# Two attentions under a gate on one Trainium2 core: the memory tokens handed on by a transpose, crosswise moves and one add

## Chip, cores and metric

One core of a Trainium2 chip (trn2). The metric is the time of one execution on the device in microseconds (us), as the median of several runs, and the kernel before and the changed kernel are compared on the same chip.

## The reference, cut to what matters

```python
g = sigmoid((x * gate_w).sum(-1, keepdims=True))           # x: 1 x 2048 x 512
a = A(x, mem0, Wq, Wk, Wv, Wo)
b = B(x, wq, wk, wv, wo, beta)
return g * a + (1 - g) * b

def A(...):                  # 32 heads of 128, M = 8 memory tokens, segments of 32 tokens
    mask = (idx[:, None] < M) | (idx[:, None] >= idx[None, :])      # over 40 tokens
    mem = mem0
    for s in range(64):
        h = concatenate([mem, x[:, 32 * s : 32 * s + 32]], axis=1)  # 40 tokens
        q, k, v = h @ Wq, h @ Wk, h @ Wv                            # 512 -> 32 x 128
        p = softmax(where(mask, q @ k.T / sqrt(128), -1e9))
        o = (p @ v) @ Wo                                            # 32 x 128 -> 512
        mem = o[:, :8]                                              # goes into the next segment
        outs.append(o[:, 8:])
...
def B(...):                  # 32 heads of 16, 4 segments of 512
    # causal softmax inside a segment, plus a linear memory (M, z) carried on
    # from segment to segment, mixed by sigmoid(beta); then @ wo
```

Attention A is a recurrence: a segment's first eight output rows are the next segment's memory tokens. Attention B and the gate depend on x alone.

## The kernel before

**A planned program.** The Python code does not emit instructions directly. Its class `Prog` collects operations, each with an engine (or a choice of engines), what it reads and writes, a cost in us and a priority. `schedule()` then replays a fixed list, the string `ORDER` at the head of the file: for every engine the sequence of its operations, found beforehand by the planner's own search over those costs (`LATENCY`, `TO_PE`, `FETCH`, `FLOOD` and the others). The list also says which engine an operation with a choice goes to. PSUM's eight banks are given out in that order; semaphores and waits are derived afterwards. So what stands in front of what on an engine is set by `ORDER`.

**Tilings of TensorE.** Most matmuls work on column groups of 32: four matmuls side by side, each on 128 x 32 weights, which the trace shows as `128*32`, in quadruples (x4). Others work on rows of 16 or 32 (`16*128`, `32*128`) or on the full array. `mm` (L1024, L1026) takes the form that fits the work before it.

**Attention A, one segment (`p_seg`).** `hT` holds the segment's 32 columns: 24 new tokens of x, copied by GpSimd (L1441), and 8 memory tokens. The last 8 tokens of each segment, the "rest", depend on no memory for their projections; they are projected for four segments at once (`p_rest`, `p_xr`) and fetched per segment.

- `wproj` (L1401) projects k, q and v in halves of 16 heads (r = 0, 1): 16 matmuls of 512 columns each half.
- k and q go out of PSUM to `st` (L1001, the general copy helper, on ScalarE or VectorE) and are transposed by VectorE (L1466) into `KT` and `QT`. v goes to `V_sb` directly.
- `p_s` makes the scores of half r in one bank, for four heads on each partition group: first the causal mask by a matmul of `neg` with `hide` over 224 columns (a L1024 x4), then 16 matmuls of 40 columns (L1481) and 4 for the rest keys (L1485) on top of it. The bank and the tile `PT` hold 4 x 40 columns and behind them 4 x 16 columns of the rest.
- L1489 takes the exponential, `p_u` sums by a matmul with ones (L1504), takes the logarithm and the exponential of its negative (L1508, L1510: 1 / sum), and multiplies (L1512 on VectorE, L1515 for the rest, mostly on GpSimd).
- L1546 and L1555 multiply the probabilities with v, giving `OT_sb`.

**The output projection (`wo`, L1300).** 64 matmuls of 256 columns collect o @ Wo in one bank. For head h, l = h mod 4 and q = l mod 2; half d of the 512 output columns goes to partitions 64 q + 32 d. So partitions 0 to 63 hold the sum over heads of even l, partitions 64 to 127 that over odd l, each as two halves of 256 columns of 32 tokens. What follows:

```python
self.copy(part, lambda: pb[so.b][:, 0:256], 256, [so], rhl, "par%s" % name, prio)   # L1001, 128 x 256 f32
...
ins = self.mm(pe, m, pb[so.b][:, 256 + 16 * c:272 + 16 * c], part[:, 128 * c:128 * c + 128], self.fold[:, :], True, True)
...
d.tensor_copy(mem[0]..., pb[so.b][:, 256:288]...)      # hm, L1323: into hT's memory columns, bf16
...
d.tensor_tensor(ao[:, :], pb[so.b][0:64, 0:256], part[64:128, :], ALU.add)     # row, L1330
```

`part` is a copy of the whole bank in SBUF. The fold, 8 matmuls of 16 columns in float32 with `fold` (a 0/1 matrix), adds the two halves, takes the eight memory tokens and turns them, in one step; each of them is two records in the trace (L1024 x16). `hm` then writes them into the next `hT`. `row` adds the halves for the output rows, and a DMA brings them to `a_rows` in DRAM (`ast`); `p_tail` reads 128 rows back, mixes them with b by the gate and writes the output. `p_orest` runs the same projection for the rest tokens of four segments, with no fold.

**Attention B** is cut into small pieces that `ORDER` strews between A's steps: logits (`bL`, L1141), exponentials (L1159, ScalarE), the causal cut (L1165, GpSimd), values (`bPV`, L1182), transposes (L1218) and so on.

**The start (`p_init`, `p_x`).** SyncE's queue holds x's four pieces first, then B's weights and A's weights; ScalarE's queue has `wBk`. The gate is 64 matmuls of one column (L934).

Of the kernel before, what the change touches and what calls it, by code (L numbers as in the profile page):

```python
# [15 lines left out]
    "c-nPZ31CcD7e061Oy<p&$t1+u5JZVctf6X;*g}I^N)<sBRiw3+Q2dR3S4)G|zLXR#B0`BqiG7c~qNOPk$;3>OH}Agx-Z#rzqQlI*dGFqH&+?t`oO{XDTA>uUH~uhX23k})eZf2@Z"  # L16
    "=DSjR>Fb@c?X-fd|dB!<4Fr&P3v_0bJkX{uoV}d{O!c0dD$mAo@mi)>MywyR%jf4<EI6^*Yx|iJ*!Id(%|=XP`CI}=%b3JkN5>OA1+<<2>jr?p+@*}-t5ta^w{)RSkiZgG5$ic-C"
    "^IucXeX3TJ`>FdU77?1ifJ1-QB5&-2<WR38onUu*q{Wq3OvEu;!2hVJ$3emO1rAcI%cy-)qR6hr~0jH<W?4-W>=E$_aS_Ax~=fY5W1sh6ROY^}ZRvTy0dLL=VoQt8e0+#Q+A!eam"
    "mF_Cv&t6Jy{zi0<eB(1Z9o1ku5VqR$W4afo3oE*Ch@Ld$@H3#~QqTYKZLouT%DCceSYJ8<Ks&x1;N9bd83$wr^DF!?MvmZadCFX2hZ18_k2+WwO80}y{iJE|1vI4dy{Ir2ia1?*k"
    "FP%vG5*AFh`)@=8NnCc#T7)p8{2I#Njbli?Ht<MlCV0E_2Lgd>Reicq#{zej<2(WYtcaYcfL=mzo<b^n`oQrt?4X=l0K|A;jYSjkffA_2MFVM6SfEMX^o@in&({YaCYOW$y`)p7D"  # L20
    "S`XiW8t_aqvKqjW{{7CHnNq!}ps?b<?`R*wI}B4o9BGDCQx}lccl|wAQsx#w{o02*@C?H*nhOpKFwQr|H)O2w?}{*(xL7i>^Ow;17;L=E6Uiuf7ORCqgCn5CVV*y)c>XNdyXQC&8"
    "+Y72_;!n^%v+zWkK>Q@Ko%!kq_yRP(Z#qJVwdIw8L)k~B$+4;xv_U_r96XPubB_I5D2!~a2}dp1JvLq@gWDhOdm=<**9v?sxJW25Ym?-ldeoxX!x`4-3l+>aiqjY*kKt=fdyyMrS"
    "TtKi`-Q|l8k2%X9cZ`c^&x5D1fH0$}`K-Y19{9|K0owjuuA~MQY~T9tV}(4D~NG=u6&MiY&(Y)ds*WfKih3Y5+XW8~DJ8n4rAi61zX|fPX3h>*sPY#?253SEIsV1Hk8!_{Fs%!nQ"
    "XbL@>yhz*P#id{eO=GyuC3I7pc!iC#F>x^|MNu9I~d942j2BKs}C{32?UUb0LFQ0ix-*wE`Wywhw40;SaxR(xH&0w&1~3r>%^+Q~*1w%X0dLK`~oRiUZ%v@YZ{<={$P$O>#Ht-g5"
    "W_?5ZV8Q)X6FKfa2uH#n*1->#gx`OOrGTS3=MBIgi05c@<lVI(bMKO(!P|IwkpyRX!0q9ky<A$_0F>qr~Z`i)*Pf7ko@^0+Ebu=O`6HS4D0zHsqF%|pCbq*x&7jftOc|B(>)Ul5$"
    "KZkl{cAySxd)nCa4`?xYI8Ydc-J`?j)*Ub>l_L53X(X=*iUSH*O)~7hZzt}07vPzsz=lT9d}LFYhY-VCz%g-Sk&Tdn#%}I-!r0;ryuSkmW=ndEhe6SCNkfQele4rTz@yN|bXC7X5"
    "{J?2%yvEGvj;w-nk4KLC-en4_WIY7iDIe*l{w;mHRx|tg>Hls*GGYd1hEQaKs1Q}WW<p1#~=%4@4Jyoy%+bJlSOafyRp_Xa4`#}?irSp1pk9MQq0GYpf9%!-z_SyD|7gBZ%B5TIq"
    "j09gbnawgKX$c#?|1Cs~gEHo!)LH84CffGH0VZT0$^?t^N$w830B|hK2#$tvh^^sW`y7ue)i_0Lx#2>;^cu>5W;-xd<!l97zIn;Kf(ek&7pZQ+7YB*SmTARuV{y-AwMMCKM1LYPP"
    "~))4IWaaGge4THwmP{^wvY!*lvJH(bT~67Xw$Rb#i-yJ6bZqrpAMCqpVq+CL^KX1>vZdW9hs0a&MX{9>MDOZ)R2yhq84)`!GpUJj{u>>cvyS0!<>j?=fe0?v}Q=Z<x@?wNUY$yZA"
    "zFPco@wd?LO2?m!oCp7uI?No{xf`T7mh(Vuka2P2NBjL6@&q4tn9-LUHbLvQ<mFTs0mU8w)fQ=)Tg95Y{pjmMvz9MhukU!<q>{^889C|HXya@J>msYn;Tl_Dv*39cH1&mo+Xe41Y"  # L30
    "-wSm-uVZSP0nU3c{&z|2*8u<9e)|_x{U6>^pl7v3#2Y5&Q0%_`roFvjdeSO!h*#aoFJaTRlWAg97R_;xOeeX3z-(9QdN}SDbR{UFCKc&eeOa*yIPK9s9P}2;t504CtmqX2Mw+iQ5"
    "@tKA=UflNik^qvi@F+4>L0)d(&!xk19$q(bRtIQWc@BSEx8e4y#yo$@6;zSCHbBOeZ<h6B!k<!-TSDxi4K*bikZ>pp~bl>Hqu#;4C5khfUzc#d<{t6?Px5m@jG!{EB_;XNdZ7Qa<"
# [1584 lines left out]
```

## Time and profile before

| | |
|---|---|
| median of 3 runs | 831.91 us (829.27 to 833.25) |
| the profiled execution | 832.89 us |
| its span in the trace | 831.2 us |
| PE (TensorE matmul) busy | 809.5 us, 97%, 24474 records |
| DVE (VectorE) busy | 617.3 us, 74% |
| ACT (ScalarE) busy | 562.9 us, 68% |
| POOL (GpSimd) busy | 260.9 us, 31% |
| granted TensorE clock | 0.998 |

A line such as `L1001 DVE CAST V_sb<-pb 128x512 bf16<-128x512 f32 x65 | 44.5, 685 | 9.9 <-PE pb L1401 9.0` is a group: the line of the kernel, the engine, the operation, the tile written and the tile read, their shapes, the count; busy us in all and mean ns of one; and the idle time of that engine just before these instructions, with what released them. PEld is TensorE's loading of weights, which runs beside the matmuls. A line of the chain of waits gives start, length, engine, tile, line and count.

### The profile page before, as it was taken

The page shows a single profiled execution, that of the slowest core. Times are in us where ns is not written, and L with a number is a line of the kernel's source. Part 1 is how long each engine was busy: PE and PEld are TensorE (multiplying, and loading weights), DVE is VectorE, ACT ScalarE, POOL GpSimd, SP SyncE. Part 2 cuts the span into 40 slices and gives each one's busy share as a digit, 9 for nine tenths or more (in the row PEclk, how much of TensorE's full clock was granted, in tenths as well). Part 3 has the DMA queues.
Part 4 walks back from the last instruction along what each step waited for, and adds up shares of the span by engine and source line. Part 5 has one row for each costly group of instructions (what it writes and reads, how often), then busy time and mean ns, then how long its engine had stood idle before and what let it go on. Part 6 is the DMA issues. An engine that isn't in the chain of part 4 may idle for free.

```text
span 831.2 us, 53272 instructions
## 1 busy us (share of the span) xinstructions
PE 809.5 (97%) x24474; PEld 521.5 (63%) x24474; DVE 617.3 (74%) x1398; ACT 562.9 (68%) x1278; POOL 260.9 (31%) x576
## 2 busy tenths in 40 slices
PE   9999999999999999999999999999999999999987
PEld 4445666666666566666666666666766665666654
DVE  4688667768778768678676687776878767886776
ACT  3577676777766667776667766676656677767663
POOL 3443231323322332323233233423232223323340
PEclk9999999999999999999999999999999999999999
DMA  9983111121111111111011111100111100000001
GB/s 341 414 247 52 40 24 43 43 45 27 43 28 28 39 28 44 27 34 44 15 47 46 38 27 31 40 14 18 44 42 32 39 20 15 13 23 23 22 21 36
DMA packets 71701, 45.63 MB, mean 55 GB/s; under 512 B 50046, under 2 KB 69942, under 8 KB 69942
## 3 DMA queue, kind: packets, MB, share of 16 engines
q1 hardware_dynamic: 70422, 41.18, 17.5%
q8 instruction: 192, 3.15, 1.6%
q10 hardware_dynamic: 1056, 1.05, 0.4%
q14 instruction: 31, 0.25, 0.1%
HBM read 30.72 MB, written 8.87 MB: 48 GB/s over the span
## 4 chain that ended last, share of the span: by engine, by line
PE 87%; DVE 4%; ACT 3%; DMA 2%; issue 1%; SPq 1%; POOL 0%; DVEq 0%; POOLq 0%
PE pb L1401 47%; PE pb L1300 17%; PE pb L1024 7%; PE pb L1141 4%; PE pb L1026 2%; PE pb L1546 2%; PE pb L1182 2%; DMA st<-in_A_mem_dram 2%; PE pb L1504 2%; PE pb L1481 1%; PE pb L1230 1%; PE pb L1555 1%; DVE KT_sb L1466 1%; PE pb L1485 1%; ACT rc_sb L1510 1%
## 5 line engine op out<-in xcount | busy, mean ns | idle before, releaser
L1001 ACT ACTIVATE st<-pb 128x512 bf16<-128x512 f32 (+2 forms) x313 | 149.0, 494 | 103.0 <-PE pb L1401 78.0
L1159 ACT ACTIVATE PTB<-pb 128x640 bf16<-128x640 f32 x240 | 158.4, 703 | 37.2 <-PE pb L1141 32.5
L1401 PE MATMUL pb<-Wv_sb,hT 128*32 128x512 bf16 x2048 | 162.8, 381 | 0.2 <-DVE ao L1330 0.2
L1401 PE MATMUL pb<-Wq_sb,hT 128*32 128x256 bf16 (+1 forms) x3072 | 138.0, 308 | 0.1
L1300 PE MATMUL pb<-Wo_sb,OT_sb 128*32 128x256 bf16 x4096 | 132.8, 273 | 3.0 <-issue 1.9
L1401 PE MATMUL pb<-Wk_sb,hT 128*32 128x512 bf16 x2048 | 132.0, 379 | 0.1
L1300 PEld LDWEIGHTS pb<-Wo_sb,OT_sb 128*32 128x32 bf16 x4096 | 100.7, 96 | 18.4 <-ACT OT_sb L1001 4.3
L1165 POOL TENSOR_SCALAR_AFFINE_SELECT PTB<-PTB 128x512 bf16<-128x512 bf16 x120 | 77.6, 647 | 107.4 <-ACT PTB L1159 100.8
L1515 POOL TENSOR_TENSOR PT_sb<-PT_sb,rc_sb 128x64 bf16<-128x64 bf16 x90 | 33.1, 367 | 248.9 <-ACT rc_sb L1510 240.5
L1401 PEld LDWEIGHTS pb<-Wq_sb,hT 128*32 128x32 bf16 x3072 | 82.5, 97 | 39.1 <-issue 0.8
L1466 DVE STREAM_TRANSPOSE QT_sb<-st 128x256 bf16<-128x256 bf16 (+1 forms) x192 | 94.4, 510 | 16.7 <-ACT st L1001 15.1
L1466 DVE STREAM_TRANSPOSE KT_sb<-st 128x512 bf16<-128x512 bf16 x128 | 89.4, 700 | 11.6 <-ACT st L1001 9.5
L1001 ACT ACTIVATE OT_sb<-pb 128x320 bf16<-128x320 f32 (+1 forms) x140 | 58.1, 428 | 37.9 <-PE pb L1555 36.3
L1401 PEld LDWEIGHTS pb<-Wk_sb,hT 128*32 128x32 bf16 x2048 | 57.0, 97 | 42.4 <-ACT PTB L1159 1.1
L1001 DVE CAST OT_sb<-pb 128x320 bf16<-128x320 f32 (+1 forms) x120 | 56.8, 478 | 31.3 <-PE pb L1555 29.3
L1401 PEld LDWEIGHTS pb<-Wv_sb,hT 128*32 128x32 bf16 x2048 | 52.2, 98 | 18.8 <-DVE ao L1330 0.7
L1508 ACT ACTIVATE rc_sb<-pb 128x160 f32<-128x160 f32 x128 | 38.8, 303 | 36.3 <-PE pb L1504 35.3
L1323 DVE CAST hT<-pb 128x32 bf16<-128x32 f32 x63 | 12.0, 191 | 66.4 <-PE pb L1024 66.1
L1489 ACT ACTIVATE PT_sb<-pb 128x224 bf16<-128x224 f32 x128 | 45.6, 356 | 17.4 <-PE pb L1485 12.8
L1001 DVE CAST V_sb<-pb 128x512 bf16<-128x512 f32 x65 | 44.5, 685 | 9.9 <-PE pb L1401 9.0
L1512 DVE TENSOR_TENSOR PT_sb<-PT_sb,rc_sb 128x160 bf16<-128x160 bf16 x128 | 42.7, 334 | 8.2 <-ACT rc_sb L1510 6.7
L1001 ACT ACTIVATE stg<-pb 128x512 bf16<-128x512 f32 (+1 forms) x68 | 37.9, 559 | 14.3 <-PE pb L1401 10.2
(203 smaller groups left out, 1472.3 us busy)
## 6 DMA issues: line engine op xcount, KB each, us to landing
Wv_sb<-in_A_Wv_dram SPq DMA_DIRECT2D x4, 1024.0 KB, 11.8
Wk_sb<-in_A_Wk_dram SPq DMA_DIRECT2D x4, 1024.0 KB, 21.0
Wq_sb<-in_A_Wq_dram SPq DMA_DIRECT2D x4, 1024.0 KB, 26.9
Wo_sb<-in_A_Wo_dram SPq DMA_DIRECT2D x4, 1024.0 KB, 20.9
rest_v<-stg SPq DMA_DIRECT2D x112, 32.0 KB
rem_v<-rest_v SPq DMA_DIRECT2D x28, 128.0 KB, 2.6
a_rows<-ao SPq DMA_DIRECT2D x63, 32.0 KB
stg<-a_rows SPq DMA_DIRECT2D x15, 128.0 KB
```

The lines of the kernel that those rows point to most:

```text
L1001: self.P.op(("act", "dve"), (lambda a: a.activation(dst, src(), ACT.Copy), lambda d: d.tensor_copy(dst, src())), reads=reads, writes=write ...
L1024: ins = pe.matmul(out[32 * c:32 * c + 32], lhsT[:, 32 * c:32 * c + 32], rhs, start=start, stop=stop, tile_position=(0, 32 * c), **kw)
L1141: ins = pe.matmul(pb[slot.banks[i]][:, base + a - lo:base + b - lo], KT[r0:r1, 128 * kc:128 * kc + 128], Q[r0:r1, t0 + a:t0 + b], start=Tr ...
L1159: P.op("act", (lambda dst=dst, src=src: lambda a: a.activation(dst, src(), ACT.Exp, scale=0.25))(), reads=[pair], writes=["%s%d_%d" % (nam ...
L1165: P.op("gp", (lambda pt=pt, ii=ii: (lambda g: g.affine_select(pt, pt, ([[0, len(ii)]] if len(ii) > 1 else []) + [[1, 128]], ALU.is_ge, 0.0 ...
L1300: ins = pe.matmul(pb[so.b][p0:p0 + 32, 0:256], tok(r, g, l), self.Wo[:, h, 256 * d:256 * d + 256], start=(r == 0 and g == 0 and l < 2), st ...
L1401: ins = pe.matmul(self.pb[sl.b][32 * g:32 * g + 32, 0:hi - lo], x[:, c, 0:32], cols, start=(c == 0), stop=(c == C - 1), tile_position=(0, ...
L1466: op("dve", (lambda dst=dst, src=src: lambda d: d.transpose(dst, src))(), reads=["st%d%s" % (i, tag)], writes=["%sT%d%s" % (kind, r, tag)] ...
L1489: op("act", lambda a: a.activation(PT[:, r, :], pb[rb.b][:, 0:224], ACT.Exp, scale=SCALE), reads=[rb], writes=["PT%d" % r, "PT%dr" % r], n ...
L1508: op("act", lambda a: a.activation(rc[:, r, :], pb[rb.b][:, 0:160], ACT.Ln), reads=[rb], writes=[rr], name="ln%d_%d" % (s, r), cost=t_act( ...
L1512: op("dve", lambda d: d.tensor_tensor(PT[:, r, 0:160], PT[:, r, 0:160], rc[:, r, :], ALU.mult), reads=[rp, rr], writes=[rp], name="nrm%d_% ...
L1515: op(("dve", "gp"), tuple((lambda e: e.tensor_tensor(rest, rest, late(rc[:, r, :]), ALU.mult)) for _ in range(2)), reads=[rp + "r", rr], w ...
```

## The change

The fold and its matrix are gone. In `wo` the two halves' columns are now taken in blocks of 32 (block index 4 bits: c, e, d; d says which half of the partitions a column goes to), and for the memory projections of odd l the order of e is reversed. VectorE transposes the bank's 128 x 256 in blocks of 32 x 32 (`turn`) into the tile `rc`, which holds 1 / sum at other times. Two `swap` copies bring 64 partitions x 32 elements each from one half of the partitions to the other, on ScalarE or GpSimd, and one VectorE add (`hm`) sums the halves into `hT`. The copy `par` now has 64 partitions in place of 128 and a priority 0.2 later; `row` adds blocks, and `p_tail` puts the columns back in order.

The mask has 160 columns in place of 224: in the scores' bank and in `PT` each head has 56 columns now, 16 of the rest and 40 of its own, and the mask is written over the 40. All readers use strided views.

x's DMAs have the first priority in the planner, `wB` loads 384 of 512 columns, the gate is 64 matmuls of 128 columns on column groups and a transpose, costs and latencies of the planner are set anew, and `ORDER` is a new list.

```diff
-    LATENCY = {"pe": 0.22, "act": 0.04, "dve": 0.04, "gp": 0.1, "sp": 2.0}
-    TO_PE = {"pe": 0.0, "act": 0.015, "dve": 0.06, "gp": 0.05, "sp": 0.0}
+    LATENCY = {"pe": 0.25, "act": 0.05, "dve": 0.05, "gp": 0.1, "sp": 2.0}
+    TO_PE = {"pe": 0.0, "act": 0.07, "dve": 0.08, "gp": 0.09, "sp": 0.0}
...
-        self.gw = t("gw_sb", [128, C])
+        self.gw = t("gw_sb", [128, C, 32])
...
-        self.hide = t("hide_sb", [128, 224])
+        self.hide = t("hide_sb", [128, 160])
...
-        self.fold = t("fold_sb", [128, 16], F32)
...
-            dma(self.g_wB[k], (lambda k: lambda s: s.dma_start(self.wB[k], self.B_w[k].rearrange("(c p) n -> p c n", p=128)))(k),
-                writes=["wB" + k], name="dma_wB" + k, prio=-102 if k == "k" else -99, load=dict(k=3.0, q=2.0, v=1.5)[k], cost=0.5, ring=4.0,
+            dma(self.g_wB[k], (lambda k: lambda s: s.dma_start(self.wB[k][:, :, 0:384], self.B_w[k].rearrange("(c p) n -> p c n", p=128)[:, :, 0:384]))(k),
+                writes=["wB" + k], name="dma_wB" + k, prio=-102 if k == "k" else -99, load=dict(k=2.7, q=1.0, v=1.0)[k], cost=0.5, ring=4.0,
...
-                  writes=[rs], name="dma_x%d_%d" % (sb, i), prio=prio - 1.5, load=0.4, cost=0.45 if sb or i else 1.2)
+                  writes=[rs], name="dma_x%d_%d" % (sb, i), prio=-110 + 0.1 * i, load=0.35 if i else 2.9, cost=0.45)
...
-            for i in range(4):
-                for c in range(C):
-                    ins = pe.matmul(pb[sg.b][:, i:i + 1], xT[:, c, i * 128:(i + 1) * 128], self.gw[:, c:c + 1], start=(c == 0), stop=(c == C - 1))
+            for c in range(C):
+                part = xT[:, c, :].rearrange("p (i b t) -> p b i t", i=4, b=4)
+                for b in range(4):
+                    ins = pe.matmul(pb[sg.b][32 * b:32 * b + 32, 0:128], self.gw[:, c, :], part[:, b], start=(c == 0), stop=(c == C - 1),
+                                    tile_position=(0, 32 * b))
...
+        def half(h, d, q):
+            w = self.Wo[:, h, :]
+            if late is None:
+                return w[:, 256 * d:256 * d + 256]
+            w = w.rearrange("p (c e d i) -> p d c e i", e=2, d=2, i=32)[:, d]
+            return w[:, :, ::-1] if mem and q else w
...
-        self.copy(part, lambda: pb[so.b][:, 0:256], 256, [so], rhl, "par%s" % name, prio)
         if mem:
-            def f_fold(pe, m):
...
+            rc = self.rc[:, :, :].rearrange("p r x -> p (r x)")
+            turned = rc[:, 0:256].rearrange("p (c e t) -> p e c t", c=4, e=2)
+            other = rc[:, 256:320].rearrange("p (c z) -> p c z", c=4)[:, :, 0:8]
+            P.op("dve", lambda d: d.transpose(rc[:, 0:256], pb[so.b][:, 0:256]), reads=[so], writes=["rc0", "rc1"], name="turn%s" % name, cost=0.45, prio=prio)
+            for e in range(2):
+                dst, src = other[64 * e:64 * e + 64], turned[64 - 64 * e:128 - 64 * e, 1, :, 24:32]
+                P.op(("act", "gp"), ((lambda a, dst=dst, src=src: a.activation(dst, src, ACT.Copy)), (lambda g, dst=dst, src=src: g.tensor_copy(dst, src))),
+                     reads=["rc0", "rc1"], writes=["rcs%d" % e], name="swap%s_%d" % (name, e), cost=(0.24, 0.24), prio=prio)
+            P.op("dve", lambda d: d.tensor_tensor(mem[0], turned[:, 0, :, 24:32], other, ALU.add),
+                 reads=["rc0", "rc1", "rcs0", "rcs1"], writes=[mem[1]], name="hm%s" % name, cost=0.23, prio=prio)
+        self.copy(part[64:128, :], lambda: pb[so.b][64:128, 0:256], 256, [so], rhl, "par%s" % name, prio + 0.2 if mem else prio)
...
+        blocks = lambda t: t.rearrange("p (c e i) -> p c e i", c=4, e=2)
+        P.op("dve", lambda d: d.tensor_tensor(blocks(ao[:, :]), blocks(pb[so.b][0:64, 0:256]), blocks(part[64:128, :])[:, :, ::-1 if mem else 1], ALU.add), reads=[so] + rhl, writes=[rao],
...
+        def by_head(t):
+            return t.rearrange("p (l q) -> p l q", l=4)
+        mine, rest = [by_head(PT[:, r, :])[:, :, 16:56] for r in range(2)], [by_head(PT[:, r, :])[:, :, 0:16] for r in range(2)]
...
-                return self.mm(pe, m, pb[rb.b][:, 0:224], self.neg[:, :], self.hide[:, :], True, True, skip_group_check=True)
+                return self.mm(pe, m, by_head(pb[rb.b][:, 0:224])[:, :, 0:40], self.neg[:, :], self.hide[:, :].rearrange("p (h q) -> p h q", h=4), True, True, skip_group_check=True)
...
-                        ins = pe.matmul(pb[rb.b][32 * g:32 * g + 32, l * L:(l + 1) * L], KT[:, 16 * r + 4 * g + l, :], QT[:, 16 * r + 4 * g + l, :],
+                        ins = pe.matmul(pb[rb.b][32 * g:32 * g + 32, 56 * l + 16:56 * l + 56], KT[:, 16 * r + 4 * g + l, :], QT[:, 16 * r + 4 * g + l, :],
...
-                    ins = pe.matmul(pb[rb.b][32 * g:32 * g + 32, 160:224], Kr[:, h0:h0 + 4].rearrange("p h k -> p (h k)"), QT[:, h0:h0 + 4, 24:40],
+                    ins = pe.matmul(by_head(pb[rb.b][32 * g:32 * g + 32, 0:224])[:, :, 0:16], Kr[:, h0:h0 + 4].rearrange("p h k -> p (h k)"), QT[:, h0:h0 + 4, 24:40],
```

In the new order the instructions that the prediction names stand at these lines: projections L1413, output projection L1310, `turn` L1329, `swap` L1332, `hm` L1334, `row` L1342, scores L1498.

201 lines of the change are left out of this document (96 added, 105 removed).

## The prediction

> **What bounds the kernel now.** I read first the page (busy shares and the chain that ended last), then the windows of the start and the end, then the chain in order of time for one hand-over between two segments.
>
> ```profile
> PE 809.5 (97%) x24474; PEld 521.5 (63%) x24474; DVE 617.3 (74%) x1398; ACT 562.9 (68%) x1278; POOL 260.9 (31%) x576
> ...
> PE 87%; DVE 4%; ACT 3%; DMA 2%; issue 1%; SPq 1%; POOL 0%; DVEq 0%; POOLq 0%
> PE pb L1401 47%; PE pb L1300 17%; PE pb L1024 7%; PE pb L1141 4%; PE pb L1026 2%; PE pb L1546 2%; PE pb L1182 2%; DMA st<-in_A_mem_dram 2%; PE pb L1504 2%; PE pb L1481 1%; PE pb L1230 1%; PE pb L1555 1%; DVE KT_sb L1466 1%; PE pb L1485 1%; ACT rc_sb L1510 1%
> ```
>
> TensorE is busy for 97% of the span and carries 87% of the chain. No other engine is above 74%. So what shortens TensorE's list of instructions, or the holes in it, shortens the kernel, and work moved to VectorE, ScalarE and GpSimd is free as long as it arrives in time.
>
> ```profile
> 0.00:62.00 62.00, 57.44 (x993) 27.82 (x994) 40.34 (x103) 34.00 (x67) 27.69 (x74) 0.97 0.92 336
> 813.00:831.20 18.20, 14.09 (x405) 8.30 (x393) 11.04 (x25) 5.88 (x17) 0.71 (x2) 1.00 0.14 40
> ```
>
> ```profile
> L1323 DVE CAST hT<-pb x63: 178/191/193, 63.9 to 813.4; 128x32 bf16<-128x32 f32 x63
> ```
>
> The columns of a window are its length, then busy time of PE, PEld, DVE, ACT and POOL, clock, DMA share and GB/s. The first 62 us load weights (DMA 0.92) with TensorE nearly full; the last 18 are one segment with little beside it. Between them lie 62 steps from one write of the memory tokens (L1323) to the next: (813.4 - 63.9) / 62 = 12.09 us each. One of them in the chain:
>
> ```profile
> 414.76 1.86 PE pb L1300 x64
> 416.62 0.86 PE pb L1401 x16
> 417.48 0.11 PE pb L1024 x16
> 417.59 0.25 PE pb L1141 x8
> 417.84 3.83 PE pb L1401 x84
> 421.68 0.10 PE pb L1024 x4
> ```
>
> The output projection (L1300) ends, TensorE does other work (L1401 of the rest tokens), the fold (L1024 x16), a piece of the other attention (L1141), then the next segment's projections. All of it is TensorE's own time. Where work lies between, the segment's recurrence is hidden. A quadruple of 512 columns costs 0.86 / 4 = 0.215 us, so columns stream at full rate, and the attention piece (320 columns in quadruples, 0.13 us of streaming) pays 0.12 for its two changes of tiling.
>
> **The fold goes (63 times).** The same hand-over in the timeline, and the two starts of the first one:
>
> ```profile
> 416.02 0.70 ACT L1159 ACTIVATE PTB<-pb 128x640 bf16<-128x640 f32 x1
> ...
> 416.44 0.39 PE L1401 MATMUL pb<-Wk_sb,xr 128*32 128x512 bf16 x4
> ...
> 416.67 0.42 DVE L1001 COPY st<-pb 128x256 f32<-128x256 f32 x1 [0.89 <-PE pb L1300]
> ...
> 417.31 0.29 PE L1024 MATMUL pb<-fold_sb,st 128*32 128x16 f32 x16
> 417.52 0.32 PE L1141 MATMUL pb<-QT,KT 16*128 16x192 bf16 x8
> 417.69 0.19 DVE L1323 CAST hT<-pb 128x32 bf16<-128x32 f32 x1 [0.60 <-PE pb L1024]
> 418.03 0.40 PE L1401 MATMUL pb<-Wk_sb,hT 128*32 128x512 bf16 x4
> ```
>
> ```profile
> 63.53 0.32 PE L1024 MATMUL pb<-fold_sb,st 128*32 128x16 f32 x16
> 63.68 0.40 PE L1024 MATMUL pb<-xT,wkB_sb 128*32 128x512 bf16 x4
> ```
>
> From start to next start a fold holds TensorE for 417.52 - 417.31 = 0.21 us, or 0.15 in the first segment; the chain gives 0.11. The value nearest to what the engine loses is the distance of starts; I take 0.19. 63 x 0.19 = 12.0 us, with 63 x 0.11 = 6.9 and 63 x 0.21 = 13.2 as ends. [...]
>
> The waits in front of the folds go as well:
>
> ```profile
> L1024 PE MATMUL pb<-fold_sb,st 128*32 128x16 f32 x1008 | 19.9, 186 | 1.6 <-ACT st L1001 1.2
> L1024 PEld LDWEIGHTS pb<-fold_sb,st 128*32 128x32 f32 x1008 | 16.0, 110 | 13.4 <-ACT st L1001 8.7 <-DVE st L1001 1.9 <-issue 0.4
> ```
>
> The weight loads stood still for 8.7 + 1.9 = 10.6 us until the copy was there; the matmuls show 1.6 us, since streaming hides a part. Ends 1.6 and 10.6; I take 4, nearer to the matmuls' row, as they are what streams.
>
> **The mask gets narrower (128 times).** Its L1024 x4 stands at 0.10 us in the chain for 224 columns; 160 columns take 160 / 224 of it. 128 x 0.10 x 64 / 224 = 3.7 us. All of it is on TensorE's list.
>
> **Strided operands.** Wo is now read in blocks of 32 columns, half of them in swapped order; the rest tokens' scores are written in runs of 16 with gaps.
>
> ```profile
> L1401 PE MATMUL pb<-Wv_sb,hT 128*32 128x512 bf16 x2048 | 162.8, 381 | 0.2 <-DVE ao L1330 0.2
> L1401 PE MATMUL pb<-Wq_sb,hT 128*32 128x512 bf16 x1024 | 67.4, 379 | 0.0
> L1485 PE MATMUL pb<-QT_sb,rem_k 128*32 128x64 bf16 x512 | 27.4, 196 | 0.0
> L1504 PE MATMUL pb<-PT_sb,ones_sb 128*32 128x64 bf16 x488 | 26.0, 193 | 0.0
> ```
>
> Wv is read in one run of 512, Wq in blocks of 32: 381 and 379 ns. L1485 reads runs of 16 and writes 64 columns in one run, L1504 writes them in runs of 16: 196 and 193. So I put these at nothing for TensorE; the swapped order itself no row shows, and its price is a rival below. VectorE's and GpSimd's products over the same strided tile get a little longer, beside TensorE.
>
> **The new hand-over.** Instead of copy, fold and cast there are a transpose out of PSUM (`turn`, VectorE), two swaps of 64 partitions x 32 (by the new order 66 on ScalarE and 60 on GpSimd) and an add (VectorE). Nearest rows:
>
> ```profile
> L1218 DVE STREAM_TRANSPOSE t_sb<-pb 128x512 f32<-128x512 f32 x32 | 22.6, 706 | 2.5 <-PE pb L1182 2.5
> L1466 DVE STREAM_TRANSPOSE QT_sb<-st 128x256 bf16<-128x256 bf16 x128 | 50.6, 415 | 4.1 <-ACT st L1001 3.4
> L1510 ACT ACTIVATE rc_sb<-rc_sb 128x160 f32<-128x160 f32 x128 | 43.0, 336 | 3.3
> L939 ACT ACTIVATE g_sb<-pb 128x4 f32<-128x4 f32 x4 | 0.7, 173 | 0.5 <-PE pb L934 0.5
> L1441 POOL COPY hT<-xT 128x96 bf16<-128x96 bf16 x64 | 17.7, 276 | 6.8 <-PE pb L1504 1.4 <-PE pb L1401 0.8
> L1108 DVE TENSOR_TENSOR MZ<-MZ,t_sb 128x17 f32<-128x17 f32 x12 | 2.0, 164 | 0.2
> L1104 DVE TENSOR_TENSOR t_sb<-pb,bd_sb 128x136 f32<-128x136 f32 x12 | 3.5, 288 | 1.0 <-PE pb L1024 0.9
> L1001 DVE CAST V_sb<-pb 128x512 bf16<-128x512 f32 x65 | 44.5, 685 | 9.9 <-PE pb L1401 9.0
> ```
>
> ```profile
> 401.20 0.34 ACT L1510 ACTIVATE rc_sb<-rc_sb 128x160 f32<-128x160 f32 x1
> 401.57 0.33 DVE L1512 TENSOR_TENSOR PT_sb<-PT_sb,rc_sb 128x160 bf16<-128x160 bf16 x1 [0.56 <-ACT rc_sb L1510]
> ```
>
> The turn has 256 elements: 0.42, as the bf16 row of that length has 415 and at 512 elements f32 has 706. A swap lies between 173 (4 elements) and 336 ns (160): 0.23, below the 276 that GpSimd takes for 96. The add of 32 elements lies between 164 and 288: 0.19. From ScalarE to VectorE pass 401.57 - 401.54 = 0.03 us; with 0.05 a step, two steps and one to TensorE are 0.15. The copy started 416.67 - 416.44 = 0.23 after TensorE had gone on to other work, and so will the turn. Sum: 0.23 + 0.42 + 0.23 + 0.19 + 0.15 = 1.22 us from TensorE's leaving the output projection to the first new projection. The trace of before needed 418.03 - 416.44 = 1.59, filled with work. So the recurrence itself gets shorter, if no queue is in the way.
>
> What covers it: in the new instruction order there stand between the two, typically, five quadruples of 512 columns and one attention piece: 5 x 0.215 + 0.25 = 1.33 us, more than 1.22. Priced like this, four of the 63 hand-overs have less cover (the least about 0.5), and lack together 1.6 us. I charge 2 us, with ends of 0 and, if a step is 0.2 longer everywhere, about 0.1 x 63 = 6.
>
> The turn adds 63 x 0.42 = 26 us to VectorE, and the order moves some 20 evictions of V to it, each 0.69 by the row above; with 617 + 26 + 14 = 657 us it is 79% busy. On VectorE the late copy for the rows is put behind the add or the turn, the segment's row store and its DMA follow it; who waits for these are the rows' bank and the tails, with a segment of time. The queue's next urgent work is the transposes of q and k, and behind them the scores:
>
> ```profile
> PEld pb L1481 <- DVE QT_sb L1466: 4.1, 14, 0.5
> L934 PE MATMUL pb<-gw_sb,xT 128*128 128x1 bf16 x64 | 2.2, 164 | 0.0
> ```
>
> This wait was 4.1 us in all; I charge 2 more, ends 0 and 8. The gate's 64 one-column matmuls, 2.2 us, become 16 quadruples of 128 columns (0.054 each, 0.9 us) and a transpose off the path: 1 us less.
>
> **The start.** x stood at the head of SyncE's queue already, ahead of the three weights for the other attention; now the memory tokens follow it and each of those three loses 128 KB. 0.39 MB at the window's 336 GB/s are 1.2 us. TensorE is filled there (57.44 of 62), so I count 1 us, ends -3 and +3 for the changed order of first work. The 18 us at the end stay.
>
> **Sum** against the profiled execution, 832.89 us (span 831.2 and 1.7 around it): -12.0 - 4 - 3.7 + 2 + 2 - 1 - 1 = -17.7, so 815.2. That execution lies 1.0 above the median of the three, 831.91; I let these agree within the spread (829.27 to 833.25) and forecast 815.0 us. The ends of the terms: -6.9 - 1.6 - 3.7 + 6 + 8 + 0 + 3 is a gain of nothing to speak of (832.89 + 4.8, only if everything goes wrong at once), and -13.2 - 10.6 - 3.7 + 0 + 0 - 1 - 3 = -31.5 gives 801.4. With half of either side's distance the likeliest case runs from 807 to 826.
>
> **Rivals.**
>
> *The gain leaks away (chance 0.10).* Fold and waits go, but TensorE then meets the next wait: the scores' or the exponentials' rows come from VectorE and ScalarE at the old pace. Then what goes is the streaming alone, 6.9 + 3.7, against 2 + 6 in new waits: 832.89 - 2.6, about 830. For it speaks that the chain's DVE and ACT shares (4% and 3%) are waits already; against it, that 12.09 us a segment are TensorE's own.
>
> *The swap comes late (0.04).* In 48 of 63 hand-overs the swap on ScalarE stands right behind an exponential of the other attention (L1159, 0.70 us). If that one starts when the turn ends, the swap is 0.6 late, less 0.11 of cover: 63 x 0.5 = 31 us, and 815 + 31 = 846. It decides from 0.39 of lateness on (17.7 / 63 + 0.11). Against it: the exponential of 416.02 was over at 416.72, and the swap is wanted at 416.67 + 0.42 = 417.09.
>
> *Strides cost streaming (0.03).* [...] Were the swapped half of the projection at half rate, 63 x 32 matmuls at 1.86 / 64 = 0.029 us more each would add 58 us: 815 + 58 = 873. [...]
>
> *More than forecast (0.10).* The fold's whole 10.6 us of waits and its 13.2 go, and the new order has fewer holes: 801 to 806.
>
> **Chances.** The forecast's own case has 0.73 and lies in 807 to 826. A measurement of this kernel can tell about 0.5%, 4.2 us: faster is below 827.8, slower above 836.1. Faster: the forecast's case, the last rival and 0.01 of the leak, 0.84. Same: 0.08 of the leak. Slower: the late swap, the strides and 0.01 of the leak, where an unfortunate order joins it, 0.08. A range from 806 to 828 leaves out these 0.16 above and some 0.04 of the last rival below.
>
> **What would show it.** Right: no fold group; TensorE busy some 15 us less; the mask's group at about 230 ns and 0.07 in the chain; L1413 and L1310 groups at the old 380 and 273 ns; hand-overs of L1334 11.8 us apart; TensorE's waits for hT under 3 us; VectorE near 79%. Wrong: a projection row above 273 ns; a wait for hT or for the swaps of 0.3 us in every segment; waits of the scores for VectorE's transposes above 12 us; a first L1334 later than 67 us.

## The result, and the profile after

The changed kernel takes 827.47 us (median of 20 runs) where the kernel before takes 831.85 in runs beside it: ratio 0.9954, interval 0.9939 to 0.9969, or 3.8 us less. Forecast were 815.0 us, 16.9 less. The sign was right; a quarter of the gain came. Below, every ratio is to runs of the kernel before that were taken beside it, and is turned into us with 831.85; verdicts rest on ratios, since single executions of one kernel differ by several us (before: 828.85 to 834.46).

The page of the changed kernel, busy time and chain:

```profile
span 824.9 us, 51903 instructions
PE 795.8 (96%) x23652; PEld 500.9 (61%) x23652; DVE 670.5 (81%) x1510; ACT 561.1 (68%) x1306; POOL 269.8 (33%) x627
PE 82%; DVE 7%; ACT 4%; DMA 2%; issue 2%; SPq 1%; POOL 1%; ACTq 0%; POOLq 0%; DVEq 0%
```

TensorE's busy time fell by 13.7 us, about as forecast, but its share of the chain from 87 to 82%, and VectorE's went from 4 to 7%. Work left TensorE and waits came. The groups of the new hand-over and of the mask, and the view of the add's line:

```profile
L1329 DVE STREAM_TRANSPOSE rc_sb<-pb 128x256 f32<-128x256 f32 x63 | 28.2, 448 | 36.4 <-PE pb L1310 36.2
L1332 ACT ACTIVATE rc_sb<-rc_sb 64x32 f32<-64x32 f32 x66 | 15.0, 228 | 33.6 <-DVE rc_sb L1329 32.3
L1332 POOL COPY rc_sb<-rc_sb 64x32 f32<-64x32 f32 x60 | 12.4, 207 | 105.4 <-DVE rc_sb L1329 101.9 <-DVE omg_sb L944 2.8
L1334 DVE TENSOR_TENSOR hT<-rc_sb 128x32 bf16<-128x32 f32 x63 | 20.5, 326 | 18.9 <-POOL rc_sb L1332 15.2 <-ACT rc_sb L1332 2.6 <-ACT st L1002 0.5
L1334 DVE TENSOR_TENSOR hT<-rc_sb x63: 182/266/752, 59.1 to 808.3; 128x32 bf16<-128x32 f32 x63
L1025 PE MATMUL pb<-hide_sb,neg_sb 128*32 128x160 bf16 x508 | 30.9, 233 | 0.1
```

Turn and swaps are as priced (0.448 for 0.42; 0.228 and 0.207 for 0.23). The add is not: 0.326 on average and up to 0.752 for 0.19. And the step from one write of hT to the next is (808.3 - 59.1) / 62 = 12.08 us, as before (12.09), not 11.8: in this execution the first write came 4.8 us earlier (the new order puts 978 of TensorE's matmul records ahead of it, the old one 1032), and the 62 steps between brought nothing.

One such hand-over in the timeline:

```profile
306.08 0.45 DVE L1329 STREAM_TRANSPOSE rc_sb<-pb 128x256 f32<-128x256 f32 x1 [0.41 <-PE pb L1310]
306.57 0.23 ACT L1332 ACTIVATE rc_sb<-rc_sb 64x32 f32<-64x32 f32 x1
306.66 0.20 POOL L1332 COPY rc_sb<-rc_sb 64x32 f32<-64x32 f32 x1 [3.04 <-DVE rc_sb L1329]
...
306.95 0.62 POOL L1217 TENSOR_TENSOR t_sb<-t_sb,rmem 128x256 f32<-128x256 f32 x1
306.97 0.65 DVE L1334 TENSOR_TENSOR hT<-rc_sb 128x32 bf16<-128x32 f32 x1 [0.44 <-POOL rc_sb L1332]
...
307.67 0.83 PE L1413 MATMUL pb<-Wq_sb,hT 128*32 128x512 bf16 x12 [0.20 <-DVE hT L1334]
```

GpSimd ends its swap and takes the next instruction of its queue (L1217), 0.02 us before the add starts. The add then lasts until 307.62, 0.05 after that instruction's end at 307.57. In 33 of the 63 segments the add is longer than 0.22 us, and in each of them a GpSimd instruction that began before it is still running; in 31 the add ends 0.04 to 0.05 us after that one. Of these 33 GpSimd instructions, 32 stand right behind a swap in GpSimd's queue. The excess over 0.193 us is 8.4 us in all. TensorE's waits for the add (matmuls, weight loads), and below them those of the scores for VectorE's transposes:

```profile
PE pb L1413 <- DVE hT L1334: 3.2, 10, 0.8
PEld pb L1413 <- DVE hT L1334: 16.4, 37, 1.3
PEld pb L1498 <- DVE QT_sb L1483: 4.0, 17, 0.5
PEld pb L1498 <- DVE KT_sb L1483: 1.8, 7, 0.5
```

There are 37 such waits of weight loads at 63 hand-overs. The prediction's sign of being right was under 3 us of waits for hT. The scores' waits, 5.8 us here, are what they were before (4.1 + 1.9).

### The profile page after: what moved, and what is told of

It is laid out like the page before. It is cut to its first block, busy times and chain, and to the rows that moved or that the text cites. A ratio compares the mean times of both kernels' runs of the same rounds, so it can differ in the third digit from the quotient of the medians.

```text
span 824.9 us, 51903 instructions
## 1 busy us (share of the span) xinstructions
PE 795.8 (96%) x23652; PEld 500.9 (61%) x23652; DVE 670.5 (81%) x1510; ACT 561.1 (68%) x1306; POOL 269.8 (33%) x627
## 4 chain that ended last, share of the span: by engine, by line
PE 82%; DVE 7%; ACT 4%; DMA 2%; issue 2%; SPq 1%; POOL 1%; ACTq 0%; POOLq 0%; DVEq 0%
PE pb L1413 46%; PE pb L1310 16%; PE pb L1025 6%; PE pb L1142 3%; PE pb L1562 2%; PE pb L1183 2%; DMA Wv_sb<-in_A_Wv_dram 2%; PE pb L1521 2%; PE pb L1498 2%; DVE hT L1334 1%; PE pb L1027 1%; DVE rc_sb L1329 1%; ACT PTB L1160 1%; PE pb L1571 1%; ACT rc_sb L1527 1%
## 5 line engine op out<-in xcount | busy, mean ns | idle before, releaser
L1002 ACT ACTIVATE st<-pb 128x512 bf16<-128x512 f32 (+2 forms) x301 | 143.6, 498 | 81.5 <-PE pb L1413 75.0
L1413 PE MATMUL pb<-Wv_sb,hT 128*32 128x512 bf16 x2048 | 155.2, 380 | 0.0
L1413 PE MATMUL pb<-Wq_sb,hT 128*32 128x256 bf16 (+1 forms) x3072 | 138.0, 308 | 1.7 <-DVE hT L1334 1.1
L1413 PE MATMUL pb<-Wk_sb,hT 128*32 128x512 bf16 x2048 | 133.9, 380 | 2.8 <-DVE hT L1334 2.2
L1310 PE MATMUL pb<-Wo_sb,OT_sb 128*32 128x256 bf16 x4096 | 130.5, 273 | 2.1 <-issue 1.4
L1310 PEld LDWEIGHTS pb<-Wo_sb,OT_sb 128*32 128x32 bf16 x4096 | 101.2, 96 | 14.6 <-issue 3.8
L1413 PEld LDWEIGHTS pb<-Wq_sb,hT 128*32 128x32 bf16 x3072 | 81.2, 97 | 47.0 <-DVE hT L1334 6.0
L1413 PEld LDWEIGHTS pb<-Wk_sb,hT 128*32 128x32 bf16 x2048 | 53.4, 96 | 51.5 <-DVE hT L1334 10.5
L1002 DVE CAST OT_sb<-pb 128x320 bf16<-128x320 f32 (+2 forms) x122 | 57.6, 477 | 23.6 <-PE pb L1571 22.4
L1002 DVE CAST V_sb<-pb 128x512 bf16<-128x512 f32 x85 | 57.8, 681 | 6.5 <-PE pb L1413 5.1
L1413 PEld LDWEIGHTS pb<-Wv_sb,hT 128*32 128x32 bf16 x2048 | 48.5, 97 | 18.2 <-ACT st L1002 0.6
L1329 DVE STREAM_TRANSPOSE rc_sb<-pb 128x256 f32<-128x256 f32 x63 | 28.2, 448 | 36.4 <-PE pb L1310 36.2
L1413 PE MATMUL pb<-Wv_sb,xr 128*32 128x512 bf16 x512 | 43.6, 381 | 4.3 <-DMA rest_v<-stg 2.2
```

What stands on the lines that cost most here:

```text
L1002: self.P.op(("act", "dve"), (lambda a: a.activation(dst, src(), ACT.Copy), lambda d: d.tensor_copy(dst, src())), reads=reads, writes=write ...
L1310: ins = pe.matmul(pb[so.b][p0:p0 + 32, 0:256], tok(r, g, l), half(h, d, q), start=(r == 0 and g == 0 and l < 2), stop=(r == 1 and g == 3 a ...
L1329: P.op("dve", lambda d: d.transpose(rc[:, 0:256], pb[so.b][:, 0:256]), reads=[so], writes=["rc0", "rc1"], name="turn%s" % name, cost=0.45, ...
L1413: ins = pe.matmul(self.pb[sl.b][32 * g:32 * g + 32, 0:hi - lo], x[:, c, 0:32], cols, start=(c == 0), stop=(c == C - 1), tile_position=(0, ...
```

## The experiments

Theory A: the add, held up by GpSimd, makes the hand-over late and keeps the gain from arriving. Rival B: what goes from TensorE's list isn't worth its face value, since something else is late next. Both turned out to hold a part.

### The hand-over

**e1**, the add with one input from PSUM.

```diff
-            d.tensor_tensor(mem[0], turned[:, 0, :, 24:32], other, ALU.add)
+            d.tensor_tensor(mem[0], <pb[so.b][:, 0:256] in the same view>, other, ALU.add)     # in ORDER: par behind hm on VectorE, 19 times
```

> The changed kernel, but the add that writes the memory columns takes its first input from PSUM (the untransposed bank, so its values are not the reference's) in place of the SBUF tile; it still waits for the turn and both swaps. In 19 segments the late copy on VectorE stands behind the add instead of before it. Theory A (the add is held by GpSimd: it ends 45 ns after the GpSimd instruction that was running, 8.4 us in all, of which 5.8 us reach TensorE as waits for hT): the add takes 0.19 us everywhere, the waits fall from 8 to about 2.5 us, and the time from 827.5 to about 821.7 us, ratio to before 0.988. Rival B (the waits for hT would only be replaced by the next wait, or the fold and the mask were worth less than was priced): the add gets short, but the time stays within 2 us of 827.5, ratio 0.995.

Measured 0.9966 (0.9946 to 0.9985): no gain over the changed kernel. The mechanism was right: at 34 of the 63 adds a GpSimd instruction was running, and none took more than 0.193 us. The waits for hT fell, and those of the scores rose:

```profile
L1334 DVE TENSOR_TENSOR hT<-pb,rc_sb 128x32 bf16<-128x32 f32 x63 | 12.0, 191 | 25.5 <-POOL rc_sb L1332 22.7 <-ACT rc_sb L1332 2.9
...
PEld pb L1413 <- DVE hT L1334: 7.4, 26, 0.8
PEld pb L1498 <- DVE QT_sb L1483: 5.5, 20, 0.7
PEld pb L1498 <- DVE KT_sb L1483: 3.8, 11, 0.8
```

**e2**, no wait for the swaps: `d.tensor_tensor(mem[0], turned[:, 0, :, 24:32], turned[:, 1, :, 24:32], ALU.add)`.

> The changed kernel, but the add takes both halves from the same partitions of the turned tile and doesn't wait for the swaps, which still run; the crosswise sum is left out. The hand-over gets 0.38 us shorter (from the end of the turn to the add: 0.44 us now, about 0.06 then). Theory A (hand-over is what keeps the gain from arriving): 7.0 of the 8.2 us of waits for hT go, time about 820.5 us, ratio 0.986. Rival B: the time stays within 2 us of 827.5.

Measured 0.9915 (0.9896 to 0.9935): 3.2 us better than the changed kernel, half of what theory A expected. This add still has two SBUF inputs and was still held in places (0.241 us on average, up to 0.658).

**e4**, two adds across partitions in place of swaps and add.

```diff
+            d.transpose(pb[so.b][:, 256:384] ..., halves(pb[so.b][:, 0:256])[:, 0])     # and half 1 into rc
+            for e in range(2): d.tensor_tensor(mem[0][64 * e:64 * e + 64], <pb, own 64 partitions>, <rc, the other 64>, ALU.add)
```

> A variant that computes the reference: VectorE transposes one half of the columns into unused columns of the same PSUM bank and the other half into SBUF, and two adds of 64 partitions each (one input PSUM, one SBUF, from the other half of the partitions) write hT; no swaps on ScalarE and GpSimd, no add with two SBUF inputs. Estimated from turn to last add: 0.27 + 0.27 + 2 x 0.19 and 0.15 of gaps, 1.07 us, where the changed kernel takes 1.21 on average and 1.8 at worst. Theory A: about 5 us less than the changed kernel, 822.5 us, ratio 0.989. Rival B: no gain, 827.5 or more (VectorE does 0.3 us more in each segment).

Measured 0.9990 (0.9976 to 1.0005), 3 us worse than the changed kernel. The transposes of half the columns took 0.329 and 0.317 us, not 0.27, and the late copy stood behind the adds as in e1.

**e7**, GpSimd held, the order unchanged. In each segment with a swap on GpSimd the next operation of GpSimd's list gets the add as one more dependency:

```diff
+        for a, b in HOLD: self.all[a].deps.append(self.all[b])      # 59 pairs: GpSimd's operation behind a swap, hm
```

> The changed kernel, computing the reference in the same order, but GpSimd's instruction behind a swap waits until the add has been done, so that it doesn't run beside the add. Theory A (the add held by GpSimd is what makes the hand-over late): the add takes 0.19 us nearly everywhere in place of 0.33 on average, the waits for hT fall from 8.2 to about 2.5 us, and the time to about 822 us, ratio 0.988. Rival B (as the first of these runs showed with the late copy moved too: the waits go over to the scores): about 827, ratio 0.995. Rival C: GpSimd's later work is missed elsewhere: over 829, ratio 0.997 or more.

Measured 0.9886 (0.9854 to 0.9917), a median of 820.71 us beside 829.70 for the kernel before: 5.6 us better than the changed kernel (some 3 us either way, by the two intervals), as theory A expected, and faster than both kernels.

```profile
L1334 DVE TENSOR_TENSOR hT<-rc_sb 128x32 bf16<-128x32 f32 x63 | 12.3, 196 | 18.9 <-POOL rc_sb L1332 15.2 <-ACT rc_sb L1332 2.6 <-ACT st L1002 0.5
PE pb L1413 <- DVE hT L1334: 0.5, 2, 0.3
PEld pb L1413 <- DVE hT L1334: 9.4, 30, 0.8
...
305.06 0.62 POOL L1217 TENSOR_TENSOR t_sb<-t_sb,rmem 128x256 f32<-128x256 f32 x1 [0.38 <-DVE hT L1334]
```

The last row is the instruction that held the add at 306.95 above; here it waits for hT instead. GpSimd, a third busy, has room for that.

**e9**, e7 with the late copy behind the add in 19 segments, as in e1.

> The kernel with GpSimd held behind the add, computing the reference, and in 19 segments the late copy on VectorE stands behind the add and not before it, as in the run where the add reads PSUM. If that shift is what gave back the gain there (its waits for the scores' operands went up by 3.5 us): about 824 us, ratio 0.993. If it was the chaining of the late copy on ScalarE behind the add that did it, or chance: no change to the held kernel, ratio 0.989.

Measured 0.9966 (0.9949 to 0.9982): the move of 19 copies by one place costs 6.6 us and explains e1. The weight loads of the scores waited 3.6 + 5.4 = 9.0 us for VectorE's transposes, as in e1 (9.3), where the changed kernel has 5.8:

```profile
PEld pb L1498 <- DVE QT_sb L1483: 5.4, 20, 0.5
PEld pb L1498 <- DVE KT_sb L1483: 3.6, 11, 0.7
```

**e15**, e7 with e2's add.


> The held kernel (GpSimd's instruction behind a swap waits for the add) in which the add doesn't wait for the swaps; the crosswise sum is left out. Its hand-over is 0.38 us shorter still. 2.5 us of waits for hT are left in the held kernel: if these cost time, about 818.5 us, ratio 0.986; if other waits take their place, 820.7, ratio 0.989.

Measured 0.9880 (0.9847 to 0.9913), no different from e7. The intervals leave some 4 us either way, so the 2 us in question can't be told; the weight loads' waits for hT did fall, from 9.4 to 1.9 us.

### What the removed work was worth

**e5 and e8**, the kernel before without the fold. In e5 one record stays in its place, in e8 the operation is taken out of the program and of `ORDER`.

```diff
-                    ins = self.mm(pe, m, pb[so.b][:, 256 + 16 * c:272 + 16 * c], part[:, 128 * c:128 * c + 128], self.fold[:, :], True, True)
+                return pe.matmul(pb[so.b][0:32, 256:272], self.neg[:, 0:32], self.hide[:, 0:16], ...)     # e5; nothing in e8
-            d.tensor_copy(..., pb[so.b][:, 256:288] ...)
+            d.tensor_copy(..., pb[so.b][:, 0:32] ...)
```

> The kernel before with the fold's 16 records replaced by one bfloat16 record of 16 columns that waits for nothing; the memory columns are cast from the untransposed bank instead, so the sum of the halves is left out. All else, the order too, is as before: it measures what the fold was worth where it stood, its work and its wait for the copy, with nothing in its place. By the prediction's terms 12.0 + 4: 815.9 us, ratio 0.981. By the distances of starts without the change of tiling that stays (0.143 us x 63 = 9.0, of which one record stays) and the stops in front of it (3.5): 12 less, 820 us, ratio 0.986. Rival: TensorE's list isn't the bound to that degree, since other waits come late when it gets shorter, or instructions aren't supplied in time: 5 us or less, ratio 0.994 or more.

> The kernel before with the fold taken out altogether, no record in its place, so that TensorE no longer stops for the copy either (in the run with one record in its place that record still waited for the copy, 3.5 us in all); the cast takes untransposed columns, so the sum of the halves is left out. It shows what work and stop were worth together. Prediction's terms, 12 + 4: 0.981. From that run's measured 0.995 and the 3.5 us of stops: 7.5 us less than before, ratio 0.991. Rival (the stops were no loss, as other waits come in their place): 0.995.

Measured 0.9951 (0.9933 to 0.9970) and 0.9942 (0.9921 to 0.9964): 4.1 and 4.8 us, where the prediction had 16. By its operands the one record of e5 waits for nothing, but it writes the bank that the copy reads, so its weight load still waited for the copy, 25 times for copies on ScalarE:

```profile
PEld pb L1318 <- ACT st L1001: 9.1, 25, 0.8
```

So the two runs differ by the stops and one record, and by 0.7 us, give or take 2.4: the stops in front of the fold were worth little, if anything.

**e6 and e10**, the mask alone: the 160-column mask and the new layout in the kernel before, and `hide` over 224 columns again in the changed kernel.

> The kernel before with the 160-column mask and the 56-column layout of the scores alone, order unchanged. Streaming that goes: 128 x 64 columns x 4 / 4 / 2.4 GHz-columns, 3.4 us by the trace's 0.215 us for four times 512 columns: 828.4 us, ratio 0.996. If strided operands cost TensorE or VectorE: 832 or more, ratio 1.000 or more.

> The changed kernel with the mask over all 224 columns again, in the new layout. By streaming 3.4 us more than the changed kernel, ratio 0.9995; by what the narrower mask brought alone in the kernel before, 1.2 us more, ratio 0.997.

Measured 0.9986 (0.9965 to 1.0008) and 0.9982 (0.9963 to 1.0002): the mask brings 1.2 us in the one (-0.7 to 2.9) and 2.3 in the other (some 2 us either way). Nothing at all is within the bounds of the first, and the 3.4 us of streaming (128 masks, each narrower by 64 columns, at the 0.215 us that a quadruple of 512 columns took) within those of the second alone.

**e11**, `self.wB[k][:, :, 0:384]` in the kernel before.

> The kernel before with only 384 of the 512 columns of the three weights of the other attention loaded at the start, 0.39 MB less, all else as before. By 336 GB/s 1.2 us earlier weights: 1 us less, ratio 0.999; if the start is not bound by the loads: 1.000.

Measured 1.0002 (0.9983 to 1.0021): nothing that shows; with 1.6 us either way, a gain of 1 us couldn't be told.

**e12 and e13**, ScalarE relieved: `m = n // 2 if u >= 3 else n` columns in the exponentials of `p_exps`, in the kernel before and in e8.

> The kernel before, but ScalarE's exponentials of the other attention take half of their columns from the fourth unit on (the other half of the probabilities is left from earlier pieces), fold in place. It frees some 55 us of ScalarE (208 x 0.27). It is the reference point for the next run; if TensorE's own list sets the time: no change, ratio 1.000 (within 0.003). If ScalarE's release of PSUM banks sets it in places: 2 to 5 us less, 0.994 to 0.998.

> The same with the fold taken out as before (no record, no stop, sum left out). The fold's removal alone brought 4.8 us where the trace puts its work and its stops at 12. If what came in its place is waits for ScalarE's evictions and exponentials (the logits of the other attention waited 2.8 us longer), this kernel is 9 us or more faster than the one with half exponentials and the fold: ratio to before 0.986 or less. If the replacement is something else (supply of instructions, VectorE, the recurrence): again about 5 us between the two.

Measured 0.9986 (0.9969 to 1.0002) and 0.9937 (0.9912 to 0.9962): the fold's removal is worth 4.1 us again. ScalarE is not what takes the place of the fold. The two pages, taken on the same chip, say how the gain comes about:

```profile
span 826.5 us, 53254 instructions
PE 804.7 (97%) x24456; PEld 520.1 (63%) x24474; DVE 617.5 (75%) x1398; ACT 511.0 (62%) x1278; POOL 260.8 (32%) x576
span 824.3 us, 51150 instructions
PE 797.0 (97%) x23397; PEld 506.9 (61%) x23418; DVE 618.5 (75%) x1398; ACT 510.9 (62%) x1278; POOL 260.6 (32%) x576
```

TensorE is busy for 7.7 us less without the fold, and idle for 5.5 us more (826.5 - 804.7 and 824.3 - 797.0). Of these 5.5, 4.0 are waits of its matmuls that nothing in the profile releases (3.9 and 7.9). The pair e11 (whose smaller loads changed nothing that shows) and e8, on that chip too, gives much the same: 8.0 less busy (803.3 and 795.3), 3.8 more idle, 2.5 of it without a releaser. These are single executions.

### The supply of TensorE's instructions

**e3 and e14**, the fold's records put back as work that nobody waits for, in the output projection and behind the second mask.

```diff
+                    if mem and (r, g) == (0, 2):          # e3, in f_wo; e14: in f_hide for r = 1, s > 0
+                        for c in range(2): ins = self.mm(pe, "c32", pb[so.b][:, 256 + 16 * c:272 + 16 * c], self.Wo[:, 0, 0:256].bitcast(F32), self.Wo[:, 0, 256:288].bitcast(F32), False, False, ...)
```

> The changed kernel with the fold's matmuls put back as pure work on TensorE: 8 float32 matmuls of 16 columns (16 records) in the midst of each output projection but the last, into unused columns, with nobody waiting for them; 63 times. It measures what the fold cost on TensorE alone. As the prediction took it, 0.19 us each: +12.0, 839.5 us, ratio 1.009. By the distance of starts where the fold stood between matmuls of the same tiling, 0.143 us: +9.0, 836.5 us, ratio 1.0055. [...]

> The changed kernel with the same 16 float32 records per segment as in the third run (63 times, into unused columns, nobody waits), but behind the second mask of each segment, mostly between projections of 512 columns and the scores, in place of the midst of the output projection. If those records cost 0.14 us each time by themselves and the rest of the 20 us was the output projection running dry of instructions (64 matmuls and 64 weight loads in 1.86 us, TensorE's waits without a releaser rose from 5.4 to 13.1 us): about 9 to 13 us more than the changed kernel, ratio 1.006 to 1.011. If the records cost 0.32 us wherever they stand: 20 us more, ratio 1.019.

Measured 1.0196 (1.0174 to 1.0218) and 1.0166 (1.0132 to 1.0200): 20 and 17.6 us more than the changed kernel, beyond both numbers of e3; and since the second place costs 17.6 too, more than the 9 to 13 us expected of it, the output projection is not the reason. In both, TensorE's waits that nothing in the profile releases rose from 5.4 us to 13.1 and 11.5. The largest in e3, and TensorE's instruction queue (packets, MB) in the kernel before, the changed one and e3:

```profile
PE pb L1310 <- issue: 8.7, 10, 1.2
...
q8 instruction: 192, 3.15, 1.6%
q8 instruction: 185, 3.03, 1.6%
q8 instruction: 193, 3.16, 1.6%
```

192 packets of 16 KB for 2 x 24474 records are one for 255 records, and they start 3.3 us apart at the least, 4.0 in the median. So something other than its work and its waits for other engines could stop TensorE: the next packet. By this reading the 20 and 17.6 us are the records themselves, 9.0 us by the distance of starts, and the 7.7 and 6.1 us more of such waits, 16.7 and 15.1 in all.

**e16, e17 and e18** shift the stream and change no work behind the first microseconds (the added matmuls are written as a loop here).

```diff
+                for _ in range(32 if i == 0 else 0): pe.matmul(pb[sw.b][0:32, 0:1], self.phiK[:, 0, 0:32], self.phiQ[:, 0:1], ...)    # 64 in e17, e18
-                return pe.matmul(pb[sw.b][:, 0:512], ...)
+                return pe.matmul(pb[sw.b][:, 0:512 if i >= 8 else 256], ...)       # 16 in e17, e18
```

> The kernel before with 32 matmuls of one column (and their 32 weight loads) added to the filler work of the first microseconds, and eight of those filler matmuls cut to 256 columns to make room; nothing else is changed. All later instructions of TensorE stand 64 places further in its stream, which is fetched 256 instructions at a time (192 packets of 16 KB for 48948 records). If the places where a packet ends were chosen by the order so as to cost little, the shift costs: waits without a releaser up from about 3.8 us (3.0 to 4.2 in four traces with this order) to 7 or more, and 3 to 8 us of time, ratio 1.004 to 1.010. If supply doesn't matter: ratio 1.000 within 0.002.

> The same with 64 such matmuls, 128 places further, half a packet. Supply theory: 3 to 8 us slower, ratio 1.004 to 1.010, with waits without a releaser of 7 us or more; the rival: 1.000 within 0.002.

> The changed kernel, 128 places further. Its order was made for its own stream, so supply theory expects it to get slower too, by 3 to 8 us: ratio 0.999 to 1.005 in place of 0.995, waits without a releaser up from 5.4 us; the rival: 0.995 within 0.002.

Measured 1.0127 (1.0103 to 1.0150), 1.0235 (1.0215 to 1.0256) and 0.9959 (0.9945 to 0.9972). Half a packet costs the kernel before 19.5 us, a quarter 10.6, both more than the 3 to 8 expected, and half a packet costs the changed kernel nothing, where supply theory expected 3 to 8. Its waits without a releaser stayed where they were (4.9, 5.4 without the shift); why is open. In e16 and e17 they are 8.6 and 14.7 us (4.2 before); in e17:

```profile
PE pb L1024 <- issue: 6.3, 10, 1.0
PE pb L1300 <- issue: 3.8, 7, 1.1
PE pb L1401 <- issue: 2.7, 4, 1.0
...
L1323 DVE CAST hT<-pb x63: 180/192/193, 63.3 to 830.6; 128x32 bf16<-128x32 f32 x63
```

The first write of hT comes at 63.3 us (63.9 before), so the start is not it: the steps are (830.6 - 63.3) / 62 = 12.38 us. Between the traces the span rises by 5.4 and 16.0 us (831.2 to 836.6 and 847.2), and the waits without a releaser by 4.4 and 10.5 of these.

The traces also show where these waits lie. Number TensorE's instructions (matmuls, weight loads and the few that only wait or branch) from 0 in order of start. Then take every stretch of over 0.1 us in which neither a matmul nor a weight load runs and for which the profile has no releaser. In the kernel before there are 7, and each stands in front of an instruction whose number leaves 193 when divided by 256. So do 13 of 15 in the changed kernel, 20 of 23 in e3 and 23 of 26 in e14; of the 161 such stretches with a releaser in these four traces, none does. So it is at one place in every 256 instructions that TensorE stops, as it would if the next packet weren't there. (In e16 and e17 a few records are missing and the place drifts to lower numbers.)

The planner reckons with this. Its constants `BLOCK = 256`, `BLOCK_AT = 195.5` and `FETCH = 3.6` (3.5 in the changed kernel) let no stretch of 256 instructions begin earlier than that many us behind the one before, once the first 52 us are over, and `ORDER` was found under this account. So the order of the kernel before is fitted to where its packets end, and a shift can undo that.

## Why the prediction was off

- **The add of the hand-over** failed. The prediction priced it by the nearest rows, 164 and 288 ns, at 0.19, and the whole hand-over at 2 us with an upper end of 6. It asked what stands in front on each queue and not who runs beside: the add reads two SBUF tiles, and GpSimd's next instruction, set free by GpSimd's own swap, gets in first. Measured: 0.326 us on average, and 5.6 us of the time (e7 against the changed kernel). The way to the add was priced low too: from the turn's end to the add's start 0.49 us on average for 0.33. What that was worth isn't shown (e15 can't tell it). The removed cast read PSUM and never took more than 0.193. The swap behind an exponential, a rival at 0.04, wasn't it: most ScalarE swaps start 0.034 us after the turn.
- **The fold's -12 and -4** failed as terms: alone, work and stops brought 4.8 us (e8). First, 0.19 was too much: where the same tiling follows, the starts are 0.144 us apart on average (0.15 in the first segment, quoted there), and the 0.21 of the other quoted row holds the change of tiling, which stays. By TensorE's busy time, 7.7 and 8.0 us less without the fold, it came near the low end of 6.9. Second, the step that what shortens TensorE's list shortens the kernel was used one for one, and the 4 for the stops on top: instead TensorE's idle time rose by 5.5 and 3.8 us, and 4.0 and 2.5 of that are waits without a releaser. Without the fold the stream is 32 instructions a segment shorter (at 255 records a packet, 184 packets for 192), so other work comes to lie where packets end, and shifts alone cost this order 10 to 20 us. The supply of instructions was a term that the prediction left out, though the planner has it. What makes up the rest of the new idle time is open; ScalarE is excluded (e13).
- **The mask's -3.7** came as 1.2 to 2.3, though its streaming went as forecast: from its start to the next instruction's it takes 0.069 us where it took 0.096, 3.5 us in all. This, too, is a term of TensorE's list that didn't come one for one.
- **The start's -1**, by smaller loads, can't be told from nothing (e11); the gate's was not measured by itself. But the first write of hT did come earlier: at 57.6 to 59.1 us in all eleven traces with the new start, at 60.4 to 63.9 in the nine with the old one. Part of that is work put off rather than saved.
- **The scores' +2** for later transposes came as nothing (6.0 us of waits before, 5.8 after).
- **Strides** were right at nothing: L1413 380 and L1310 273 ns as before. From start to the next instruction's start, the 64 matmuls of an output projection, half of which read Wo in swapped blocks, take 1.757 us before and 1.758 after (medians), and the four of the rest's scores, now written to PSUM in runs of 16 with gaps, 0.032 and 0.031. The half rate of the rival on strides, 0.029 us more for each matmul of the swapped half, shows in no run.
- **The rival of the leak** comes nearest to what happened, with 830 us at a chance of 0.10: the fold and its waits went, new waits took their place. But it named the scores, and their waits rose only where the late copy was moved (e1, e9). With the parts as measured, -4.8 - 1.2 to 2.3 + 5.6 gives -0.4 to -1.5, if parts of two kernels may be added. The other 2 to 3 us are within the intervals of the parts, and what is left of the change, start, gate, queue and order, wasn't measured by itself. That the time still lies inside 806 to 828 is due to the width of the range: two terms of it were off by some 11 and 4 us, the same way.

## What to carry to other kernels

When a step leaves PSUM for SBUF, look beside it as well as ahead of it: here a VectorE add with two SBUF inputs ended 0.04 to 0.05 us behind a GpSimd instruction that began before it in 31 of 63 segments, and one added dependency a segment was worth 5.6 us, where the whole change brought 3.8. In a kernel whose order was found by search, a saved instruction need not be worth its time: take the part out alone and measure. Here a shift of the stream (10.6 and 19.5 us) or of 19 copies by a place in their queue (6.6 us) moved the time more than the edits themselves.

## Hardware that was not expected

The add against GpSimd: it took 0.65 us beside one of 0.62, in 31 of 33 slow cases it ended 0.04 to 0.05 us after the GpSimd instruction, and it never took more than 0.193 with one input in PSUM, though GpSimd was running at 34 of those adds (e1). Four adds don't fit: they ended 0.11 to 0.13 us before the GpSimd instruction that began ahead of them did (L1215 and L1360, twice each). What holds the add in the chip, no trace here shows.

TensorE's stream came in 192 packets of 16 KB for 48948 records, one for 255 and 3.3 us apart at the least. Its waits without a releaser stand at one place in every 256 instructions (7 of 7 in the kernel before, 13 of 15 in the changed one), and a shift by 128 places cost one order 19.5 us of 832 (e17) and another nothing (e18).

GpSimd's swap starts 0.13 us after the end of VectorE's turn in 42 of 60 cases, ScalarE's 0.034 in 55 of 66 (306.66 and 306.57 above, after 306.53).
